# K and Q turned on VectorE instead of TensorE for the last pairs of a chunk-select attention followed by a hardswish MLP

## The chip, the cores and the metric

The kernel runs on one core of a Trainium2 chip. The metric is the device time of one execution in microseconds (us). A core has TensorE (PE; its weight loads are listed as PEld), VectorE (DVE), ScalarE (ACT), GpSimd (POOL) and SyncE (SP, which issues DMAs here). Each engine works through its own instructions in program order and waits for others by semaphores.

## The reference

Attention with selection of key chunks, over 4 batches of 8 heads with 768 positions and a head dimension of 64, and then an MLP with a hardswish gate over the 3072 tokens (512 to 2048 to 512). All arrays are float32.

```python
k_chunks = k.reshape(B, H, nc, chunk, D)                  # chunk = 32, nc = 24
k_min, k_max = np.min(k_chunks, axis=3), np.max(k_chunks, axis=3)
ub = np.sum(np.maximum(q[:, :, :, None, :] * k_min[:, :, None, :, :],
                       q[:, :, :, None, :] * k_max[:, :, None, :, :]), axis=-1)
ub = np.where(causal, ub, -1000000000.0)
top_chunks = np.argsort(ub, axis=-1)[..., -top_k:]        # top_k = 6
scores = scale * np.matmul(q, k.transpose(0, 1, 3, 2))
mask = sel & (pos[:, None] >= pos[None, :])               # sel: key's chunk is a top chunk
attn = softmax(np.where(mask, scores, -1000000000.0))
x = np.matmul(attn, v)                                    # heads side by side: [3072, 512]
h = x @ w_in
out = (h * np.clip(h + 3.0, 0.0, 6.0) / 6.0) @ w_out
```

The bound of a query and a chunk can be computed by two matrix products, since max(q kmin, q kmax) = relu(q) kmax - relu(-q) kmin.

## The kernel before

**Tiling.** Two heads of a batch form a pair, 16 pairs in all (i = 0 to 15, four per batch). The two heads (e = 0, 1) of 64 dimensions stand on the upper and lower 64 partitions. Queries below 192 (Q0) see at most six chunks and need no selection; the other 576 (NQ) are handled in two halves h of 288 (HQ). The MLP works on 8 groups g of 384 tokens, two per batch.

**Order.** The whole schedule is a list of tokens, ORDER, written out by hand; each token emits a few instructions, and every engine runs its share of the list in that order. The tokens, with the line under which the profile shows their instructions:

- lk, lq, lv: loads of K, Q, V of a pair, issued on SP (K and Q: L215, two DMAs each, rows of 256 bytes, 768 rows per DMA). K and Q each have a ring of three buffers (KSM, QS).
- K.i.c, Q.i.c: six TensorE transposes of 128x128 float32 blocks into a PSUM slot a, b or c (L298). kb, qb: casts to bf16 on ACT (L319, L329). mx, mn: maximum and minimum per chunk on DVE, into KM (L344). rp: relu(q) on ACT (L350). rn or ra: relu(-q), on DVE (L354) or ACT (L358).
- U, or ud for two pairs at once: the bounds by matmul (L367, L391); ub or us: add the causal bias on DVE, into UBM (L372, L396). ud.6, ud.8, ud.10, ud.12, ud.14 each serve two pairs.
- T: TensorE transposes of the bounds into PSUM slot x or y (L403, L408); t8: twelve DVE instructions, each finding the eight largest of 32 (L413); sel: compare with the sixth largest (L417); L: TensorE transposes back (L427); mt: copy the mask rows to MTM (L431, L436).
- Pairs 0 to 5 add the mask to the scores by matmul (L479, with EM holding E_VAL). Pairs 6 to 15 store it to DRAM (sm, L444, four DMAs) and load it spread over partitions (ml, L449, six DMAs), cut it causally on POOL (am, L456), and multiply the exponentials by it on DVE (mu, L463).
- S, ex: scores on TensorE (L471), exponential on ACT (L485). af: causal cut on POOL (L492).
- A, B: products with V into slot x or y (L508), na, nb: divide by the sum on DVE, into XB (L525, L528).
- xt: DMA transposes of XB to XT on SP (L534), three per group; groups 0 and 1 use TensorE (X, L541) and a DVE copy (xe, L545) instead.
- H.g.f.c: first MLP product into a slot a, b or c (L552), hu: relu(h + 3) on ACT (L560), gt: min with 6 and multiply by h on DVE (L563), which frees the PSUM slot. O.g.t.n: second product into slot x or y (L590), ot: copy out on ACT (L597), st: store on SP (L603).

PSUM has three slots of two banks (a, b, c: PBa, PBb, PBc in the profile) and two of one bank (x, y: PSx, PSy). A slot is written again only when its reader is through.

Of the kernel before, what the change touches and what calls it, by code (L numbers as in the profile page):

```python
# [15 lines left out]
P = 128  # L16
# [3 lines left out]
E_VAL = 8192.0  # L20
# [15 lines left out]
Q.1.b T.0.x mn.1 t8.0 sel.0 lq.2 Q.2.a lk.2 lv.0 lq.3 lk.3 lv.1 rp.1 qb.1 ra.1 U.1.c ub.1 lk.4 vc.0 lv.2 lq.4  # L36
rp.2 qb.2 ra.2 K.2.b kb.2 L.0.y mt.0 S.0.1.c ex.0.1 S.0.2.a T.1.x S.0.3.c ex.0.2 ex.0.3 S.0.5.a ex.0.5 mx.2 mn.2
S.0.0.b ex.0.0 t8.1 sel.1 U.2.c ub.2 S.0.4.a ex.0.4 L.1.y Q.3.b rp.3 mt.1 S.1.1.c ex.1.1 qb.3 T.2.x t8.2 rn.3
K.3.a kb.3 af.0.5 af.0.3 af.0.0 af.0.1 A.0.y S.1.0.c ex.1.0 mx.3 sel.2 mn.3 S.1.4.b ex.1.4 S.1.2.c ex.1.2 L.2.x
S.1.5.b ex.1.5 vc.2 af.0.2 S.1.3.a ex.1.3 U.3.c mt.2 S.2.2.b ex.2.2 S.2.0.a ex.2.0 af.1.0 na.0 af.1.1 ub.3 T.3.x  # L40
t8.3 af.1.3 sel.3 af.2.2 af.1.5 K.4.c lq.5 kb.4 mx.4 S.2.3.b Q.4.a ex.2.3 B.0.0.y L.3.x mt.3 rp.4 lk.5 wl.0 lv.4
lq.7 S.2.1.b ex.2.1 vc.1 wc.0 af.2.0 af.1.2 af.2.1 B.0.1.y qb.4 mn.4 A.1.x S.3.1.b ex.3.1 S.3.2.c ex.3.2 S.2.5.b
ex.2.5 rn.4 U.4.a nb.0 S.3.0.c ex.3.0 na.1 ub.4 S.2.4.b ex.2.4 T.4.y t8.4 sel.4 K.5.a kb.5 mx.5 S.3.5.c ex.3.5
Q.5.b B.1.0.x L.4.y rp.5 mt.4 qb.5 B.1.1.x mn.5 S.4.2.c af.3.0 ex.4.2 rn.5 A.2.y lv.3 S.3.3.a ex.3.3 af.2.5 lk.7
lk.6 lq.8 lq.6 vc.3 wl.2 S.4.1.b U.5.c na.2 nb.1 ub.5 ex.4.1 vc.4 af.3.2 af.2.3 S.4.3.a ex.4.3 af.4.3 af.3.5
af.3.3 bd af.3.1 S.4.4.b ex.4.4 wc.2 af.4.1 af.4.2 T.5.y S.4.0.c S.3.4.a B.2.0.x S.4.5.b ex.4.0 ex.4.5 af.4.0
af.4.5 t8.5 sel.5 ex.3.4 L.5.y mt.5 B.2.1.x nb.2 lv.5 S.5.1.c ex.5.1 S.5.2.b X.0.0.y A.3.x na.3 xe.0.0 K.6.a
wl.1 lk.8 af.5.1 wc.1 ex.5.2 lk.9 wl.4 kb.6 mx.6 S.5.3.c ex.5.3 Q.6.b mn.6 B.3.0.x X.0.1.y xe.0.1 rp.6 qb.6
B.3.1.x rn.6 S.5.5.c ex.5.5 nb.3 K.7.a kb.7 mx.7 S.6.1.b ex.6.1 mn.7 Q.7.c X.1.0.y rp.7 qb.7 rn.7 S.5.0.b
B.4.0.x B.4.1.x nb.4 ex.5.0 S.6.2.a ex.6.2 af.5.2 wl.3 S.7.0.c S.5.4.b A.4.x ex.5.4 ud.6.a S.6.0.b xe.1.0 na.4  # L50
ex.7.0 us.6 X.1.1.y S.7.1.c ex.6.0 xe.1.1 lq.9 T.7.x t8.7 S.6.4.a ex.7.1 ex.6.4 S.6.3.b ex.6.3 T.6.y sel.7 t8.6
sel.6 H.1.2.c hu.1.2 gt.1.2 af.5.0 af.5.3 af.5.5 af.7.0 S.6.5.a ex.6.5 af.7.1 vc.5 af.6.0 H.1.3.b L.6.x L.7.y
mt.6 mt.7 hu.1.3 gt.1.3 K.8.a wc.4 wl.6 kb.8 wc.3 wc.6 Q.8.c rp.8 qb.8 A.5.x B.5.0.y mx.8 mn.8 rn.8 H.1.0.b
hu.1.0 gt.1.0 K.9.a kb.9 mx.9 mn.9 H.0.1.c hu.0.1 gt.0.1 B.5.1.y H.1.4.b hu.1.4 H.1.1.a hu.1.1 sm.6 Q.9.c rp.9
gt.1.4 qb.9 gt.1.1 wl.5 rn.9 sm.7 ml.6.1 wc.5 af.6.1 ml.6.4 ml.6.3 lv.6 vc.6 am.6.4 H.0.6.b hu.0.6 gt.0.6 na.5
H.0.5.a hu.0.5 ud.8.c us.8 H.0.4.b gt.0.5 wl.7 T.8.x t8.8 ml.6.0 ml.6.5 am.6.3 wc.7 ml.6.2 lk.10 lk.11 hu.0.4
gt.0.4 nb.5 S.8.0.c ex.8.0 H.0.0.a ml.7.5 am.6.5 am.6.2 hu.0.0 gt.0.0 H.0.2.c hu.0.2 gt.0.2 H.0.3.b S.7.3.a
T.9.y hu.0.3 lq.10 ml.7.4 ml.7.2 ml.7.3 sel.8 gt.0.3 H.0.7.c ex.7.3 t8.9 hu.0.7 mu.6.5 gt.0.7 ml.7.1 lq.11
S.7.4.a ex.7.4 S.8.3.b ex.8.3 O.0.0.0.x O.0.0.1.x am.7.3 am.7.5 am.7.2 am.7.4 ml.7.0 S.7.2.a S.8.4.c S.8.5.b
# [36 lines left out]
H.5.2.b hu.5.2 O.3.0.0.y O.3.0.1.y ml.14.2 gt.5.1 B.12.0.x B.12.1.x gt.5.2 nb.12 S.15.2.c ex.15.2 S.15.0.a
S.15.1.b am.14.2 O.3.0.2.y ex.15.0 ex.15.1 B.13.0.x B.13.1.x ml.15.2 ml.15.5 ml.15.0 S.15.3.c ex.15.3 ml.14.5
# [17 lines left out]
def kernel(  # L115
# [536 lines left out]
```

## Time and profile before

| | us |
|---|---|
| Time, median of 2 runs (lowest, highest) | 282.94 (282.64, 283.25) |
| Span of the profiled execution | 282.4 |
| PE / DVE / ACT / POOL busy in it | 271.8 / 195.1 / 182.1 / 72.1 |
| Six K or Q transposes on PE, in the chain | 0.66 to 0.84 |
| 12 DVE maxima of 32 (mean of one, overlapped) | 1.27 (0.177) |
| DVE select, 96x384 | 0.55 |
| Landing of a K or Q load, median | 5.0 |

The granted TensorE clock is 1.00 throughout. Matmuls are pipelined, so a busy PE is not PE at its peak: the mean of one matmul contains time in which the one before it still runs. Engine idle time is listed with what ended it. The chain that ended last is followed back from the last instruction, at each step to what released it.

### The profile page before, as it was taken

The numbers are of one execution on the slowest core, as the hardware profiler recorded it, in microseconds if no ns is written. First come the engines' busy times: TensorE is split into PE (matmuls) and PEld (weight loads), VectorE is DVE, ScalarE is ACT, GpSimd is POOL, SyncE is SP. The second block draws the span as 40 slices with busy tenths as digits, with TensorE's granted clock in tenths as the row PEclk, the third lists the DMA queues.
The fourth block names the chain that finished last, engine by engine and source line by source line (L and its number), as shares of the span: only waits on it lengthen the run. The fifth ranks groups of instructions, "written<-read, shape, count | busy, mean of one in ns | idle before, by whom it ended". The sixth has DMA issues, their size and how long they took to land.

```text
span 282.4 us, 6943 instructions
## 1 busy us (share of the span) xinstructions
PE 271.8 (96%) x2706; PEld 164.7 (58%) x2706; DVE 195.1 (69%) x523; ACT 182.1 (64%) x242; POOL 72.1 (26%) x138
## 2 busy tenths in 40 slices
PE   8798999899999999998999999999999999999995
PEld 3566777757654666564556566645456646555544
DVE  4787786979898896568975798737935894532330
ACT  2699999988758988452888865753657433433331
POOL 6034294486254031005531120107004100000000
PEclk9999999999999999999999999999999999999999
DMA  8999999979979998599999789998789320111023
GB/s 167 218 201 214 269 218 245 281 230 311 272 227 284 245 195 195 150 273 264 251 278 207 146 183 206 257 294 164 206 255 267 97 40 37 39 56 62 15 75 111
DMA packets 107056, 54.39 MB, mean 193 GB/s; under 512 B 86928, under 2 KB 96144, under 8 KB 107024
## 3 DMA queue, kind: packets, MB, share of 16 engines
q1 hardware_dynamic: 105456, 53.56, 77.8%
q10 hardware_dynamic: 1568, 0.39, 0.7%
q8 instruction: 21, 0.34, 0.6%
q14 instruction: 11, 0.09, 0.1%
HBM read 42.34 MB, written 9.24 MB: 183 GB/s over the span
## 4 chain that ended last, share of the span: by engine, by line
PE 73%; DMA 8%; ACT 5%; SPq 5%; DVE 4%; issue 2%; POOL 1%; ACTq 0%
PE PSy L590 13%; PE PSx L590 11%; PE PBb L552 10%; PE PBa L552 8%; PE PBc L552 8%; ACT PT L485 4%; DMA WS<-in_moe_w_in_dram 3%; PE PSx L508 3%; DMA QS<-in_q_dram 3%; DMA KSM<-in_k_dram 3%; PE PSy L508 2%; PE PBa L298 2%; PE PBc L471 2%; SPq L449 2%; PE PBb L290 2%; PE PBa L471 2%
## 5 line engine op out<-in xcount | busy, mean ns | idle before, releaser
L552 PEld LDWEIGHTS <-WIN 128*128 128x128 bf16 x512 | 48.9, 98 | 32.8 <-issue 1.3
L590 PEld LDWEIGHTS <-GT 128*128 128x128 bf16 x368 | 34.4, 98 | 37.9 <-issue 2.5
L590 PE MATMUL PSy<-WOUT,GT 128*128 128x512 bf16 x208 | 50.5, 379 | 0.0
L590 PE MATMUL PSx<-WOUT,GT 128*128 128x512 bf16 x160 | 38.9, 379 | 0.0
L552 PE MATMUL PBb<-XT,WIN 128*128 128x384 bf16 x192 | 35.1, 326 | 0.0
L485 ACT ACTIVATE PT<-PBc 128x1024 bf16<-128x1024 f32 (+2 forms) x34 | 31.4, 924 | 3.9 <-PE PBc L471 3.2
L485 ACT ACTIVATE PT<-PBb 128x1024 bf16<-128x1024 f32 (+2 forms) x35 | 31.3, 895 | 3.8 <-PE PBb L471 2.0
L456 POOL TENSOR_SCALAR_AFFINE_SELECT WS<-WS 128x256 bf16<-128x256 bf16 x30 | 12.5, 427 | 71.6 <-DMA WS<-SCR 51.8
L560 ACT ACTIVATE U<-PBb 128x768 bf16<-128x768 f32 x24 | 19.5, 811 | 16.3 <-PE PBb L552 16.3
L552 PE MATMUL PBa<-XT,WIN 128*128 128x384 bf16 x160 | 29.3, 326 | 0.0
L563 DVE SCALAR_TENSOR_TENSOR GT<-U,PBb 128x768 bf16<-128x768 bf16 x24 | 22.8, 950 | 9.4 <-ACT U L560 9.1
L552 PE MATMUL PBc<-XT,WIN 128*128 128x384 bf16 x160 | 29.3, 326 | 0.0
L508 PEld LDWEIGHTS <-PT 128*128 128x128 bf16 x672 | 24.8, 98 | 6.1 <-POOL PT L492 1.7
L463 DVE TENSOR_TENSOR PT<-PT,WS 128x256 bf16<-128x256 bf16 (+2 forms) x70 | 27.4, 441 | 0.0
L485 ACT ACTIVATE PT<-PBa 128x1024 bf16<-128x1024 f32 (+2 forms) x27 | 25.8, 954 | 2.0 <-PE PBa L471 1.3
L563 DVE SCALAR_TENSOR_TENSOR GT<-U,PBa 128x768 bf16<-128x768 bf16 x20 | 19.0, 950 | 10.6 <-ACT U L560 10.5
L563 DVE SCALAR_TENSOR_TENSOR GT<-U,PBc 128x768 bf16<-128x768 bf16 x20 | 19.0, 950 | 10.4 <-ACT U L560 10.4
L492 POOL TENSOR_SCALAR_AFFINE_SELECT PT<-PT 128x256 bf16<-128x256 bf16 x56 | 22.2, 420 | 11.6 <-ACT PT L485 11.5
L560 ACT ACTIVATE U<-PBa 128x768 bf16<-128x768 f32 x20 | 16.3, 813 | 13.5 <-PE PBa L552 13.3
L293 POOL CAST VB<-VS 128x768 bf16<-128x768 f32 x16 | 13.5, 850 | 44.5 <-DMA VS<-in_v_dram 44.5
L471 PEld LDWEIGHTS <-KB 64*128 64x128 bf16 x320 | 14.4, 94 | 14.6 <-issue 10.3
L560 ACT ACTIVATE U<-PBc 128x768 bf16<-128x768 f32 x20 | 16.2, 812 | 9.9 <-PE PBc L552 9.6
(125 smaller groups left out, 396.3 us busy)
## 6 DMA issues: line engine op xcount, KB each, us to landing
VS<-in_v_dram SPq DMA_DIRECT2D x16, 384.0 KB, 5.0
KSM<-in_k_dram SPq DMA_DIRECT2D x31, 192.0 KB, 5.0
QS<-in_q_dram SPq DMA_DIRECT2D x31, 192.0 KB, 5.0
out_dram<-OT SPq DMA_DIRECT2D x23, 256.0 KB, 2.3
WS<-in_moe_w_in_dram SPq DMA_DIRECT2D x4, 1024.0 KB, 8.6
WS<-in_moe_w_out_dram SPq DMA_DIRECT2D x4, 1024.0 KB, 6.2
SCR<-MTM SPq DMA_DIRECT2D x40, 72.0 KB, 3.5
WS<-SCR SPq DMA_DIRECT2D x10, 288.0 KB, 5.5
```

The source lines that it names most:

```text
L290: nc.tensor.matmul(PSB[c][:, 0, :], lhsT=WARM[:, 0:P], rhs=WARM, start=True, stop=True)
L293: nc.gpsimd.tensor_copy(VB[i % 4][:, :, :, 0:D], VS[i % 2][:].rearrange("p e j d -> p j e d"))
L456: nc.gpsimd.affine_select(out=T, in_=T, pattern=[[0, 2], [1, P]], compare_op=A.is_ge, fill=0.0, base=0, channel_multiplier=-1)
L463: nc.vector.tensor_tensor(out=T, in0=T, in1=mask_view(i, j, lo, q0 + n), op=A.mult)
L471: nc.tensor.matmul(PSB[c][:, e, at:at + n], lhsT=K[rows, j * P:(j + 1) * P], rhs=Q[rows, q0:q0 + n], start=True, stop=q0 + n <= Q0 or i in ...
L485: nc.scalar.activation(PT[i % 3][u][:, :, 0:n], PSB[slot["S", i, u]][:, :, 0:n], ACT.Exp, scale=float(scale))
L492: nc.gpsimd.affine_select(out=T[:, :, lo:lo + P], in_=T[:, :, lo:lo + P], pattern=[[0, 2], [1, P]], compare_op=A.is_ge, fill=0.0, base=0, ...
L508: nc.tensor.matmul(O[:, e, t, :], lhsT=PT[i % 3][u][:, e, lo:lo + P], rhs=VB[i % 4][:, j, e, :], start=(j == 0), stop=(j == qb))
L552: nc.tensor.matmul(PSB[c][:, ff, 0:GRP], lhsT=WIN[:, kt, (2 * f + ff) * P:(2 * f + ff + 1) * P], rhs=XT[g % 3][:, kt, :], start=(kt == 0), ...
L560: nc.scalar.activation(slot["R", g, f][:], PSB[slot["H", g, f]][:, :, 0:GRP], ACT.Relu, bias=3.0)
L563: nc.vector.scalar_tensor_tensor(out=GT[g % 2][:, 2 * f:2 * f + 2, :], in0=slot["R", g, f][:], scalar=6.0, in1=PSB[slot["H", g, f]][:, :, ...
L590: nc.tensor.matmul(PSS[c][:], lhsT=GT[g % 2][:, f, t * P:(t + 1) * P], rhs=WOUT[:, f, :], start=(f == 0), stop=(f == FT - 1))
```

## The change

K and Q of pairs 10 to 15 (tokens kd, qd in place of K, Q) are loaded by load_turned: four DMAs per tensor, each to 32 partitions, in rows of 32 float32 (128 bytes), so that a DVE transpose of 32x32 blocks, in place in SBUF, gives the layout that TensorE gave before. The casts and reductions then read SBUF instead of PSUM. For these pairs the second part of the bound is q times the minimum (negation dropped), and the first is relu(q) times the maximum less the minimum, for which kx subtracts the two on DVE; relu(-q) is no longer made. The K casts of pairs 11, 13 and 15 go from ACT to POOL (kp).

For pairs 6 to 15 the selection of two pairs at once stays on DVE: tr (block transpose of the bounds, 128x576), tm (18 maxima instead of 24), se (one compare), tb (block transpose of the mask). The tokens T, t8, sel, L and mt of these pairs go. tr, tm, se and tb stand directly behind us of their pair of pairs. Everything else in ORDER keeps its place; kd and qd stand where K and Q stood.

For pairs 0 to 5, E_VAL and the compare change sign, so that mt is a plain copy.

```diff
-E_VAL = 8192.0
+E_VAL = -8192.0
...
-ex.7.0 us.6 X.1.1.y S.7.1.c ex.6.0 xe.1.1 lq.9 T.7.x t8.7 S.6.4.a ex.7.1 ex.6.4 S.6.3.b ex.6.3 T.6.y sel.7 t8.6
-sel.6 H.1.2.c hu.1.2 gt.1.2 af.5.0 af.5.3 af.5.5 af.7.0 S.6.5.a ex.6.5 af.7.1 vc.5 af.6.0 H.1.3.b L.6.x L.7.y
-mt.6 mt.7 hu.1.3 gt.1.3 K.8.a wc.4 wl.6 kb.8 wc.3 wc.6 Q.8.c rp.8 qb.8 A.5.x B.5.0.y mx.8 mn.8 rn.8 H.1.0.b
...
+S.7.0.c S.5.4.b A.4.x ex.5.4 ud.6.a S.6.0.b xe.1.0 na.4 ex.7.0 us.6 tr.6 tm.6.0 tm.6.1 se.6 tb.6 X.1.1.y S.7.1.c
+ex.6.0 xe.1.1 lq.9 S.6.4.a ex.7.1 ex.6.4 S.6.3.b ex.6.3 H.1.2.c hu.1.2 gt.1.2 af.5.0 af.5.3 af.5.5 af.7.0 S.6.5.a
+ex.6.5 af.7.1 vc.5 af.6.0 H.1.3.b hu.1.3 gt.1.3 K.8.a wc.4 wl.6 kb.8 wc.3 wc.6 Q.8.c rp.8 qb.8 A.5.x B.5.0.y mx.8
...
+sm.6 Q.9.c rp.9 gt.1.4 qb.9 gt.1.1 wl.5 rn.9 sm.7 ml.6.1 wc.5 af.6.1 ml.6.4 ml.6.3 lv.6 vc.6 am.6.4 H.0.6.b hu.0.6
+gt.0.6 na.5 H.0.5.a hu.0.5 ud.8.c us.8 tr.8 tm.8.0 tm.8.1 se.8 tb.8 H.0.4.b gt.0.5 wl.7 ml.6.0 ml.6.5 am.6.3 wc.7
+ml.6.2 lk.10 lk.11 hu.0.4 gt.0.4 nb.5 S.8.0.c ex.8.0 H.0.0.a ml.7.5 am.6.5 am.6.2 hu.0.0 gt.0.0 H.0.2.c hu.0.2
...
+ex.8.2 mu.6.4 O.0.1.0.y H.1.7.b hu.1.7 A.6.x na.6 kd.10 kd.11 gt.1.7 kb.10 kp.11 mx.10 mx.11 mn.10 kx.10 mn.11 kx.11
+B.6.0.x O.0.1.1.y qd.10 O.0.1.2.y O.0.1.3.y B.6.1.x rp.10 qb.10 ot.0.1 st.0.1 sm.8 st.0.0 lk.12 nb.6 S.9.3.a S.9.5.c
+S.9.2.b ex.9.3 mu.7.4 mu.7.3 mu.7.1 mu.7.0 ex.9.5 ex.9.2 O.0.2.0.y O.0.2.1.y qd.11 O.0.2.2.y rp.11 qb.11 O.0.2.3.y
+S.9.4.c ex.9.4 ot.0.2 ud.10.b S.9.0.a S.9.1.c lv.8 ex.9.1 mu.7.2 mu.7.5 ex.9.0 sm.9 A.7.x B.7.0.y us.10 tr.10
+tm.10.0 tm.10.1 se.10 tb.10 na.7 xt.2 B.7.1.y st.0.2 nb.7 S.10.1.c ex.10.1 S.10.4.b S.10.0.a ml.9.2 ml.8.3 ml.8.1
...
+    def load_turned(dst, x, i):
+        b, hp = divmod(i, NPAIR)
+        for e in range(2):
+            for d in range(2):
+                g = D * e + CH * d
+                nc.sync.dma_start(dst[g:g + CH].rearrange("p (n d) -> p n d", d=CH),
+                                  x[b, 2 * hp + e].rearrange("(n t) d -> t n d", t=CH)[:, :, CH * d:CH * (d + 1)])
...
+    def turn_k(i):
+        nc.vector.transpose(out=KF[i % 3], in_=KF[i % 3])
...
+    def k_span(i):
+        T = KM[i % 3][:, :, 0:NCH]
+        nc.vector.tensor_tensor(out=T[:, 0], in0=T[:, 0], in1=T[:, 1], op=A.subtract)
...
+    def turn_double(i):
+        nc.vector.transpose(out=UBT[:], in_=UBD.rearrange("p e n -> p (e n)"))
+
+    def top8_double(i, e):
+        view = UBT[:].rearrange("p (s c) -> p s c", c=CH)
+        for s in range(9 * e, 9 * e + 9):
+            nc.vector.max(out=T8D[:, s, :], in_=view[:, s, :])
+
+    def select_double(i):
+        nc.vector.tensor_tensor(out=SELD[:], in0=UBT[:].rearrange("p (s c) -> p s c", c=CH),
+                                in1=T8D[:, :, TOPK - 1:TOPK].to_broadcast([P, 2 * HQ // CH, CH]),
+                                op=A.is_ge if i in PRODUCT else A.is_lt)
+
+    def turn_back(i):
+        nc.vector.transpose(out=MTD[(i // 2) % 2].rearrange("p e n -> p (e n)"), in_=SELD[:].rearrange("p s c -> p (s c)"))
```

## The prediction

> **What bounds the kernel now.** I read the page first: engine totals and slices.
>
> ```profile
> PE 271.8 (96%) x2706; PEld 164.7 (58%) x2706; DVE 195.1 (69%) x523; ACT 182.1 (64%) x242; POOL 72.1 (26%) x138
> ...
> PE   8798999899999999998999999999999999999995
> ...
> DVE  4787786979898896568975798737935894532330
> ...
> DMA  8999999979979998599999789998789320111023
> ```
>
> PE is occupied everywhere, DMA until slice 31 (about 220 us). The chain that ended last agrees (73% PE), but it leaves PE in two places that the change touches, waiting for the loads of Q 12 and K 13:
>
> ```profile
> 123.20 0.54 SPq L215
> 123.80 7.47 DMA QS<-in_q_dram
> 131.41 0.84 PE PBb L298 x6
> ...
> 144.78 7.13 DMA KSM<-in_k_dram
> 152.04 0.84 PE PBa L298 x6
> ```
>
> PE stood still only 0.80 and 0.15 us there, so PE's work and the loads arrive nearly together: taking PE work away gains little unless the load comes earlier too. Then the timeline around the four places where the change puts selection work on DVE in one piece. Columns: start, length, engine, line, operation.
>
> ```profile
> 60.91 0.76 DVE L396 TENSOR_TENSOR UBM<-PBa,BIASM 128x576 f32<-128x576 f32 x1 [0.57 <-PE PBa L391]
> ...
> 61.58 0.55 DVE L545 COPY XT<-PSy 128x768 bf16<-128x768 bf16 x1
> ...
> 63.09 1.46 PE L552 MATMUL PBc<-XT,WIN 128*128 128x384 bf16 x8
> ...
> 79.80 0.76 DVE L396 TENSOR_TENSOR UBM<-PBc,BIASM 128x576 f32<-128x576 f32 x1
> ...
> 80.47 0.94 DVE L563 SCALAR_TENSOR_TENSOR GT<-U,PBa 128x768 bf16<-128x768 bf16 x1
> ...
> 81.68 1.47 PE L552 MATMUL PBa<-XT,WIN 128*128 128x384 bf16 x8
> ```
>
> Each time the bias add (us) is followed on DVE at once by something PE needs within two microseconds: the last copy into XT before H.1.2, and the gate that frees PBa for H.0.0. At 108.38 (us.10) the two normalisations follow, the second at 110.36; PSy is written again at 113.60 (O.1.2.0).
>
> **What goes.** On PE, 12 groups of six K or Q transposes at 0.66 us (their pieces in the chain), 10 groups T at 0.35 (starts 159.77, 160.14, 160.47) and 10 groups L at 0.13 (165.67, 165.80, 165.92): 7.9 + 3.5 + 1.3 = 12.7 us. On ACT, five negative parts (0.67) and three K casts (0.80): 5.8 us; the casts go to POOL, 0.85 each by its row for VB. On DVE, 10 x (12 maxima 1.27 + select 0.55 + mask 0.30) = 21.2 us and one negative part, 0.76.
>
> **What comes on DVE.** No row shows a block transpose. Of 128x768 f32 I bound it by the 128x768 bf16 copy, 0.55 us, and by twice the 128x768 f32 reduction, 1.9; I take the reduction's own 0.95, the same shape passed once. Selection of a double pair: transpose of 128x576 f32 0.76 (the row of us; bounds 0.42 to 1.5), 18 maxima at 0.105 (12 took 1.27) 1.9, select 0.76, bf16 transpose 0.45 (between copies of 288, 0.30, and of 768, 0.55): 3.9 us in one unbroken block. Five blocks, 19.5, replace the 21.2; twelve turns add 11.4 and six subtractions of 24 columns 0.6. DVE's total rises by about 10 us; that is not the point. The point is where each piece stands in DVE's order.
>
> Costed at nothing: the casts on POOL for pairs 11 and 15 (POOL is 26% busy; the scores of these pairs come several us later; without that cover 0.85 each), the source of casts and reductions (SBUF for PSUM: the PSUM rows stand, 0.80 and 0.95; a gain is possible, of a tenth or so by their pace), and the sign in pairs 0 to 5 (mask row 0.30 as copy, 0.305 with the subtraction). ACT's 5.8 us are a gain only where ACT is waited for; at pair 10 it is, and the wait for DVE there is longer.
>
> [...]
>
> **What comes on the queues.** Each of 12 loads is four DMA issues instead of two. An issue of 768 packets takes about 0.55 us on SP (1.12 for two at 123.20): +1.1 us of SP per tensor. Packets double to 3,072 and halve to 128 bytes. From 5 to 10 us only 256-byte packets run:
>
> ```profile
> DMA packets 4338, 1.09 MB, mean 218 GB/s; under 512 B 4338, under 2 KB 4338, under 8 KB 4338
> ```
>
> That is 5 us x 16 / 4338 = 18.4 ns of an engine per packet. Rows of 2 KB reach some 430 GB/s near 53 us, 76 ns per packet. A line through both gives 14.3 ns for 128 bytes: 2.75 us per tensor against 1.77. The bounds are 1.77 (cost by bytes) and 3.53 (cost by packets). I take the middle between 1.77 and the line, about +0.5 us, for the sum and the rest for the range.
>
> [...]
>
> **The sum, against the profiled span of 282.4** (the runs' median, 282.94, is 0.5 above it). I follow the order through and say by how much PE is late (+).
>
> Pair 6/7: us.6 ends 61.67, block to 65.6, xe.1.1 to 66.1; H.1.2 starts there instead of 63.09: +3.0; L.6, L.7 gone: +2.7. Until then PE has only two groups of scores, under 1 us.
>
> Pair 8/9: us.8 ends 83.3, block to 87.2, gt.0.5 to 88.1; H.0.0 needs PBa: 88.1 instead of 81.68, +6.4. T.9, L.8, L.9 gone: +5.8 at A.6.
>
> Turns of 10 and 11: na.6 ends at 103.0 (97.22 before). Then in order on DVE kd.10, kd.11 (1.9), gt.1.7 (0.95), four reductions (3.6), two subtractions (0.2), qd.10 (0.95): 110.6. ACT waits in order at rp.10 for that, then qb.10, then ot.0.1, which frees PSy: 112.7; O.0.2.0 starts there instead of 102.46. PE's saved 2.0 us (K.10, K.11, Q.10) is lost in the wait. ud.10 needs qd.11 and rp.11: 116.3 instead of 107.0, +9.3. The loads are covered: lk.10 and lk.11 are issued from 83.58 on and need some 3 us longer than before, kd.10 comes at 103. Were that cover gone, each late microsecond would add one.
>
> Pair 10/11: us.10 ends 118.4, block to 122.3, na.7 and nb.7 to 123.8; O.1.2.0 at 123.8 instead of 113.60, +10.2. xt.2 waits for na.7, so H.2.7 is equally late.
>
> Q 12: SP goes on from xt.2 (issue ends 127.0) through one store and nine mask loads (6.6 us as before) and four issues (2.2) to 135.8; the load lands 7.5 us later, 143.3; qd.12 ends 144.3. PE no longer waits for it, but na.8 and gt.2.5 queue behind it on DVE, and B.8 and S.11.5 behind those: +9.
>
> K 13: lq.13 costs SP 1.1 more; lk.13 is issued with +10 and +1.1 more, lands at about 164 (152.0 before); kd.13, then kp.13 on POOL, 165.8; S.13.0 was at 153.96: +11.8. ud.12 some +11.5.
>
> Pair 12/13: us.12 ends 170.2, block to 174.1, na.11 to 174.9; xt.4 must wait for na.11, 3.8 of issue, 2.5 to land: 181.2. H.4.0 was at 167.22: +14.
>
> Pairs 14, 15: SP issues 17 DMAs in place of 9 (8.3 us before), kd.15 waits for the last; gt.4.4 and O.4.2.2 queue behind kd.15, two reductions, qd.15, kd.14. 2.65 us of PE is saved, and about as much lost in these waits. T and L of these pairs (0.96) go, and block 14 is covered by O.4.1, H.3.7, H.3.4 and O.4.0 (some 8 us of PE): +13. From 215 us on nothing changes and PE is full, so the delay reaches the end: 282.9 + 13 = about 296.
>
> Of the 13, the four blocks give 3.0, 3.7, 1 and 2.5 (10), the turns of 10/11 3.5, the later loads about 3.5; 4 come back as saved PE work. With turns at 0.55 us, blocks at 3.1 and packets at no more than their bytes, the same walk gives +7, 290; with turns and blocks' transposes doubled and packets at full price, +24, 307.
>
> **Rivals.** *PE is relieved (faster).* The end is set by PE in 73% of the chain; 12.7 us of its work goes, to 270. It needs DVE's blocks to be hidden: DVE is 31% idle, but at 61, 80 and 109 us the follower is wanted within 2 us. It decides if a block takes under 2 us. *Paid back (no change).* The waits of about 13 use up the 12.7 once: 283; for it speaks that PSUM banks a to c come free earlier and PE finds work at the blocks; against, that PE's order is fixed. *128-byte packets set it (slower still).* At 3.53 us per tensor or more and DMA full from 120 to 155, the late loads of 12, 13, 14 and 15 add 6 to 8: 303. *It doesn't do what it says:* a 4-byte turn takes two passes, 1.9 us; DVE then holds ud.10, Q 12, K 13 and 15 some 9 us longer: 305. This one is in the upper range.
>
> **The numbers.** My walk 0.60, packets or two-pass turns 0.16, paid back 0.15, relieved 0.09. The likeliest gives 296. The range 284 to 308 takes in the bounds of the unknown costs and the upper part of "paid back". About 2% is what a measurement here can tell from no change: slower 0.77 (nearly all of the first two), same 0.14, faster 0.09.
>
> **What would show it.** H.1.2 starting 3 us after the last maximum of pair 6, H.0.0 right behind a gate that follows tb.8; PE idle of several microseconds near 63, 84, 105, 118 and 178; ACT waiting for DVE at rp.10; DVE waiting for a load at qd.12, kd.13, kd.15; turns in rows of 0.95 us; loads of K and Q with over 5 us to land. I'm wrong if PE goes on without gaps at 62 to 66, or if the turns cost less than half.

## The result and the profile after

The changed kernel takes 310.03 us (median of 309.46 and 310.60) against 282.94: a ratio of 1.0978, 95% interval 1.0877 to 1.1079. The direction was forecast, the size was not: +27 us came where +13 was expected, 2 us above the upper end of the range. The profiled execution has a span of 307.7 us (before 282.4) and a mean granted clock of TensorE of 0.967 (before 1.000). The kernels below are compared with up to 17 runs of the kernel before, median 282.5. Executions of one kernel mostly spread by 1 to 5 us, so differences of one microsecond between times are not read.

From the page of the changed kernel, engine totals and slices (each 7.7 us):

```profile
PE 269.2 (87%) x2554; PEld 155.3 (50%) x2574; DVE 207.4 (67%) x505; ACT 177.2 (58%) x234; POOL 75.6 (25%) x141
...
PE   8798999939949956989879897949999999999995
...
DVE  3777887866895497684986887894785496342430
...
PEclk9999999978997995999999999997999999999999
DMA  9999999989989703749899956979978840030112
```

PE has four holes (slices 9, 12, 15 and 27, counted from 1), and the row PEclk, which was all nines before, drops in or right after each of them. The busy time of PE fell by only 2.6 us, though 12.7 us of its work was taken out. Most of the rest went into slower matmuls: the granted clock is at half for 20.5 us in all (65.3 to 72.1, 92.6 to 96.0, 116.5 to 123.3 and 208.7 to 212.1), and PE works in 17.1 of them, which loses 8.5. After slice 28 PE is full, as before.

The four holes in the timeline of PE (start, length, operation, in brackets the idle time before it and its releaser):

```profile
67.06 2.08 PE L556 MATMUL PBc<-XT,WIN 128*128 128x384 bf16 x6 [4.82 <-DVE XT L549]
...
91.63 1.79 PE L556 MATMUL PBa<-XT,WIN 128*128 128x384 bf16 x8 [4.25 <-DVE GT L567]
93.22 2.77 PE L556 MATMUL PBc<-XT,WIN 128*128 128x384 bf16 x8
...
118.17 4.42 PE L594 MATMUL PSy<-WOUT,GT 128*128 128x512 bf16 x10 [5.00 <-ACT OT L601]
...
207.82 2.81 PE L594 MATMUL PSy<-WOUT,GT 128*128 128x512 bf16 x8 [4.16 <-DVE GT L567]
```

The releasers are those of the prediction: the copy into XT behind block 6, the gate behind block 8, ot.0.1 behind the turn of Q 10, gt.4.4 behind the turns of pairs 14 and 15. For the last two, the rows of ScalarE and VectorE show the turns ahead of them (rp.10 waits for the turn, ot.0.1 follows at 117.53; a turn, then gt.4.4):

```profile
116.22 0.68 ACT L337 ACTIVATE RP<-QS 128x576 f32<-128x576 f32 x1 [5.72 <-DVE QS L239]
...
205.99 0.93 DVE L236 STREAM_TRANSPOSE KSM<-KSM 128x768 f32<-128x768 f32 x1
206.85 0.91 DVE L567 SCALAR_TENSOR_TENSOR GT<-U,PBb 128x768 bf16<-128x768 bf16 x1
```

The lengths of the matmuls are not as predicted: eight of an H group took 1.46 to 1.47 us before and take 2.77 at 93.22. The windows of 5 us show it as the granted clock (the column with no count, 0.53 and so on, after the busy times of PE, PEld, DVE, ACT and POOL):

```profile
65.00:70.00 5.00, 2.94 (x10) 1.10 (x10) 1.97 (x3) 0.83 (x2) 2.50 (x2) 0.53 0.70 253
70.00:75.00 5.00, 5.00 (x52) 3.65 (x50) 2.83 (x4) 3.40 (x5) 1.89 (x1) 0.79 0.79 245
...
115.00:120.00 5.00, 1.83 (x5) 0.69 (x5) 4.93 (x13) 3.78 (x6) 0.00 (x0) 0.65 0.16 57
120.00:125.00 5.00, 4.95 (x32) 1.82 (x35) 0.94 (x3) 2.25 (x4) 0.00 (x0) 0.67 0.61 142
```

And the first hole from the side of VectorE, with GpSimd's row that lies beside it. The block is 60.82 to 66.56, 5.74 us where 3.9 was costed:

```profile
60.82 0.78 DVE L395 STREAM_TRANSPOSE UBT<-UBM 128x576 f32<-128x576 f32 x1
61.63 1.77 DVE L400 MAX8 T8D<-UBT 128x8 f32<-128x32 f32 x18
63.44 2.31 DVE L403 TENSOR_TENSOR SELD<-UBT,T8D 128x576 bf16<-128x576 f32 x1
65.78 0.78 DVE L408 STREAM_TRANSPOSE MTM<-SELD 128x576 bf16<-128x576 bf16 x1
66.48 0.52 DVE L549 COPY XT<-PSy 128x768 bf16<-128x768 bf16 x1
...
63.25 1.89 POOL L252 CAST WOUT<-WS 128x2048 bf16<-128x2048 f32 x1
```

How late PE is against the profile before, read from the first weight load of matmul groups that both kernels have (us):

| place | predicted | after |
|---|---|---|
| H.1.3 and H.1.1, behind block 6 | +3.0 | +4.7, +5.9 |
| O.0.0.0, behind block 8 | +6.4 | +11.5 |
| O.0.2.3, behind the turns of 10 and 11 | +10.2 | +17.3 |
| O.1.2.0, behind block 10 | +10.2 | +17.5 |
| O.2.2.0, behind Q 12 | +9 | +20.1 |
| O.2.1.1, behind K 13 | +11.8 | +20.4 |
| H.4.5, behind block 12 | +14 | +22.0 |
| O.3.1 and all that follows | +13 | +25.0 |

Two things lie under all such figures. Within the first 10 us, where the kernels are the same, the profiles already differ by up to 1.3 us (against the profile before: changed kernel +0.3, filled stalls −0.5, one stall +0.1, one stall filled −1.0). And the profile before waits 1.3 us for GpSimd at 57 us, which most others don't, so that they seem some 1.1 us less late than they are. Growth from row to row is free of both; where two runs are compared below, the difference of their starts is named.

The theory to be tested after this: the stalls are the predicted ones, but each long one is paid twice, once as waiting and once in the half-rate matmuls after it. The rivals: the 128-byte loads, or VectorE too full as such.

### The profile page after: what moved, and what is told of

It reads as the page before. It is cut to its first block, busy times and chain, and to the rows that moved or that the text cites. A ratio compares the mean times of both kernels' runs of the same rounds, so it can differ in the third digit from the quotient of the medians.

```text
span 307.7 us, 6684 instructions
## 1 busy us (share of the span) xinstructions
PE 269.2 (87%) x2554; PEld 155.3 (50%) x2574; DVE 207.4 (67%) x505; ACT 177.2 (58%) x234; POOL 75.6 (25%) x141
## 4 chain that ended last, share of the span: by engine, by line
PE 51%; DVE 16%; issue 9%; ACT 8%; DMA 8%; SPq 5%; POOL 2%; DVEq 0%; ACTq 0%; POOLq 0%
PE PSx L594 8%; PE PSy L594 7%; PE PBa L556 7%; PE PBb L556 7%; PE PBc L556 6%; ACT PT L489 5%; DVE KM L329 4%; DMA VS<-in_v_dram 3%; SPq L220 3%; DVE GT L567 3%; PE PSx L512 2%; DMA out_dram<-OT 2%; PE PBb L286 2%; PE PSy L512 2%; DMA KSM<-in_k_dram 2%
## 5 line engine op out<-in xcount | busy, mean ns | idle before, releaser
L556 PEld LDWEIGHTS <-WIN 128*128 128x128 bf16 x512 | 50.1, 100 | 50.4 <-issue 19.2
L594 PEld LDWEIGHTS <-GT 128*128 128x128 bf16 x368 | 35.5, 100 | 54.3 <-issue 14.8
L594 PE MATMUL PSy<-WOUT,GT 128*128 128x512 bf16 x198 | 52.1, 400 | 11.0 <-ACT OT L601 5.0
L594 PE MATMUL PSx<-WOUT,GT 128*128 128x512 bf16 x150 | 37.9, 386 | 0.6 <-issue 0.2
L556 PE MATMUL PBb<-XT,WIN 128*128 128x384 bf16 x192 | 36.5, 335 | 0.6 <-ACT PT L489 0.5
L556 PE MATMUL PBc<-XT,WIN 128*128 128x384 bf16 x160 | 31.7, 343 | 5.5 <-DVE XT L549 4.8
L567 DVE SCALAR_TENSOR_TENSOR GT<-U,PBb 128x768 bf16<-128x768 bf16 x24 | 22.8, 948 | 12.5 <-ACT U L564 12.2
L460 POOL TENSOR_SCALAR_AFFINE_SELECT WS<-WS 128x256 bf16<-128x256 bf16 x30 | 12.9, 439 | 66.9 <-DMA WS<-SCR 66.8
```

The costliest lines, as they stand in the source:

```text
L460: nc.gpsimd.affine_select(out=T, in_=T, pattern=[[0, 2], [1, P]], compare_op=A.is_ge, fill=0.0, base=0, channel_multiplier=-1)
L556: nc.tensor.matmul(PSB[c][:, ff, 0:GRP], lhsT=WIN[:, kt, (2 * f + ff) * P:(2 * f + ff + 1) * P], rhs=XT[g % 3][:, kt, :], start=(kt == 0), ...
L567: nc.vector.scalar_tensor_tensor(out=GT[g % 2][:, 2 * f:2 * f + 2, :], in0=slot["R", g, f][:], scalar=6.0, in1=PSB[slot["H", g, f]][:, :, ...
L594: nc.tensor.matmul(PSS[c][:], lhsT=GT[g % 2][:, f, t * P:(t + 1) * P], rhs=WOUT[:, f, :], start=(f == 0), stop=(f == FT - 1))
```

## The experiments

**The change in two halves.** One run has only the selection's part, the other only the turned K and Q.

```diff
 # selection only: K, Q, their loads, casts and parts as before
-ud.6.a ... us.6 ... T.7.x t8.7 ... T.6.y sel.7 t8.6 sel.6
+ud.6.a ... us.6 tr.6 tm.6.0 tm.6.1 se.6 tb.6 ...
 # turning only: T, t8, sel, L, mt as before
-K.10.a K.11.c gt.1.7 kb.10 kb.11 mx.10 mx.11 mn.10 mn.11
+kd.10 kd.11 gt.1.7 kb.10 kp.11 mx.10 mx.11 mn.10 kx.10 mn.11 kx.11
```

> The kernel before with only the selection of pairs 6 to 15 moved to VectorE, in one block behind each bias add as in the change; K and Q of pairs 10 to 15 stay on TensorE. Theory (the blocks hold up what TensorE waits for, and each stall of over 4 us is followed by some 5 us at half the matmul rate): the two stalls before H.1.2 and H.0.0 come back with the slow matmuls behind them, 294 to 298 us. Rival (the 128-byte loads set the loss): no loss here, 278 to 284 us.

> The kernel before with only K and Q of pairs 10 to 15 turned on VectorE (128-byte loads, kd, qd, kx, casts on GpSimd); the selection stays on TensorE. Theory: the stalls before O.0.2.0 (pairs 10/11) and O.4.2.2 (pairs 14/15) remain, 290 to 297 us, and the two losses add up to the whole (27 us). Rival (each part alone finds slack and only both together lose): under 287 us.

Selection only: 298.4 us, ratio 1.061 (1.0543 to 1.0678), +16; the two stalls come back, 3.17 us before H.1.2 and 5.61 before H.0.0. Turning only: 294.9, ratio 1.0432 (1.0387 to 1.0476), +12.4, with stalls of 4.99 us before O.0.2.0 and 4.17 before O.4.2.2. Together they make 28.3, against 27 for the whole change: the halves add up, and the larger one is the selection, of which the prediction had said 10 less the work that PE is spared. Where each half is late: selection only is +3.2 at H.1.1, +9.8 at O.0.0.0, +11.2 at O.1.2.1 and +12.9 at H.4.5; turning only (its profile is of the longest of its four executions, 298.3 us) is ahead by about 2 until O.0.2.0, which is the difference of the starts and of the wait at 57 us alone, then +3 at O.0.2.1, +4.7 at O.2.2.0, +8.9 at O.2.1.3 and +13 from O.3.1 on.

**The same blocks, put later.** The whole change, with each block cut in pieces that stand behind the copy or gate that PE waits for.

```diff
-us.6 tr.6 tm.6.0 tm.6.1 se.6 tb.6 ... xe.1.1 ... gt.1.2
+us.6 ... xe.1.1 tr.6 tm.6.0 tm.6.1 ... gt.1.2 se.6 tb.6
-us.8 tr.8 tm.8.0 tm.8.1 se.8 tb.8 ... gt.0.5 ... gt.0.4 ... gt.0.0 ... gt.0.2 ... gt.0.3
+us.8 ... gt.0.5 tr.8 ... gt.0.4 tm.8.0 ... gt.0.0 tm.8.1 ... gt.0.2 se.8 ... gt.0.3 tb.8
```

Blocks 10 and 12 likewise, behind nb.7, gt.1.6 and gt.2.7, and behind na.11, gt.3.6 and gt.3.5; block 14 stayed.

> The changed kernel with the same instructions, the four blocks tr, tm, se, tb of pairs 6, 8, 10 and 12 cut into two to five pieces and moved behind the copy, gates and normalisations that TensorE waits for. Theory: the stalls before H.1.2 and H.0.0 and their slow matmuls go, 295 to 299 us. Rival (VectorE is simply too full, so the work costs the same wherever it stands): 306 us or more.

297.4 us, ratio 1.0499 (1.0437 to 1.0562): the place alone is worth some 12.5 us, since the instructions are the same. For the selection this speaks against the rival that VectorE is too full as such. The first two holes are gone, the other two stand:

```profile
108.10 2.26 PE L593 MATMUL PSy<-WOUT,GT 128*128 128x512 bf16 x5 [4.99 <-ACT OT L600]
...
195.18 3.60 PE L593 MATMUL PSy<-WOUT,GT 128*128 128x512 bf16 x8 [4.16 <-DVE GT L566]
```

**The clock: the holes filled.** Two runs put matmuls of constants into the holes, so that PE waits as long but is not idle.

```diff
+    def busy(c, n):
+        flat = EM[:].rearrange("p j h x -> p (j h x)")
+        for _ in range(n):
+            nc.tensor.matmul(PSS[c][:] if c in "xy" else PSB[c][:, 0, :], lhsT=IDENTB[:], rhs=flat[:, 0:512],
+                             start=True, stop=True)
...
-H.1.2.c ... H.0.0.a ... S.9.3.a S.9.5.c S.9.2.b ... O.0.2.0.y ... O.4.2.2.y
+ZX.x.22 H.1.2.c ... ZX.x.18 H.0.0.a ... ZX.c.22 S.9.3.a S.9.5.c S.9.2.b ... O.0.2.0.y ... ZX.a.18 O.4.2.2.y
```

That is the second of the two; in the first, the third set was 80 matmuls of 128 columns into slot c, directly ahead of O.0.2.0.

> The changed kernel with idle matmuls (identity by a constant, into columns of PSUM that nobody reads) put into the four long TensorE stalls, before H.1.2, H.0.0, O.0.2.0 and O.4.2.2. Theory (after 4 us of an idle TensorE its granted clock is halved for about 5 us): the stalls keep their length, the matmuls behind them run at full rate, 299 to 303 us. Rival (the slow matmuls come from what runs beside them, memory traffic or VectorE): they stay slow, 309 to 312 us.

It missed: 311.7 us, ratio 1.1042 (1.1009 to 1.1075), in the range of its rival, though the matmuls behind the first two holes ran at a clock of 1.00. At O.0.0.0 PE was only +6.15 late instead of +11.5 (1.0 of the difference is in the starts), but the third set had to wait 6.82 us for an exp that still read slot c, started at 114.60 and ran into the time when O.0.2.0 was free to go; +18.1 followed. The fill had become a delay of its own, so it was made again with that set ahead of S.9.3, where slot c is empty.

> The changed kernel with matmuls of constants (512 columns each, results never read) put into its four long stalls; unlike in the first try, the third set goes ahead of S.9.3 into slot c, which nothing is waiting to read there. Nothing of the reference is left out. Theory (a stall of PE of over 4 us makes the matmuls after it run at half rate, and this is 8 to 10 us of the 27): granted clock 1.00 throughout, 300 to 303 us, O.0.2.0 no later than +11 instead of +16. Rival (the slow matmuls do not lie on the path, since the waits behind them are for DVE, ACT and loads): 307 to 310 us, as the changed kernel.

Its four executions took 303.64 and 304.0 us at a granted clock of 1.00 and 0.994, and 310.99 and 312.7 at 0.983 and 0.978, so no ratio can be given: the fill kept the clock up in two of them, and why not in the other two is open. In the profiled one (303.64, span 301.9) the groups behind the first two holes run at full pace:

```profile
66.25 1.14 PE L562 MATMUL PBc<-XT,WIN 128*128 128x384 bf16 x6 [0.22 <-DVE XT L555]
...
88.44 1.46 PE L562 MATMUL PBa<-XT,WIN 128*128 128x384 bf16 x8 [0.26 <-DVE GT L573]
89.74 1.46 PE L562 MATMUL PBc<-XT,WIN 128*128 128x384 bf16 x8
```

1.14 us for six instead of 2.08, though the block ahead of them is as long as in the changed kernel (its select takes 2.32). PE is +6.75 at O.0.0.0 (after: +11.5), +10.25 at O.0.2.3 (+17.3), +19.1 at the end (+25.0). Of each difference 0.8 us is there before the first hole. The fourth fill gained nothing; a stall of 1.25 us for gt.4.4 stayed. So some 5 us of the 25 went with the clock in this execution. Because the executions differ, the same question was put to the kernel before, with one hole and nothing else.

```diff
+    def hold(n):
+        for _ in range(n):
+            nc.vector.tensor_reduce(out=IDLE[:], in_=BIASM[:].rearrange("p (c w) -> p c w", w=CH),
+                                    axis=AX.X, op=A.max)
...
-us.6 X.1.1.y S.7.1.c ex.6.0 xe.1.1
+us.6 X.1.1.y S.7.1.c ex.6.0 ZD.16 xe.1.1
 # in the twin also
-T.6.y ... H.1.2.c
+ZX.c.22 T.6.y ... H.1.2.c
```

> The kernel before with 16 reductions of a constant on VectorE (about 0.37 us each, their results never read) ahead of xe.1.1: one stall of TensorE of some 5 us at 62.7 us and nothing else; everything is computed. Theory (a stall of this length is followed by matmuls at half rate): the 8 matmuls of H.1.2 behind it take over 2.4 us instead of 1.46, TensorE is later by the stall and about 2 us more, 289 to 291 us. Rival (the stall alone counts): H.1.2 in 1.46 us, 287 to 288 us.

> As the run with one stall, with 22 matmuls of constants into slot c (4.8 us, results never read) where TensorE would stand still. Theory: H.1.2 in 1.46 us, granted clock 1.00 in the stretch, about 2 us less than its twin. Rival (the clock has no part in it): the same time as its twin.

The reductions took 7.78 us, 0.49 each instead of the expected 0.37, so the hole is longer than meant, 7.1 us. The stall alone and its window:

```profile
68.78 0.88 PE L407 MATMUL PSy<-IDENT,UBM 128*96 128x128 f32 x3 [7.08 <-DVE XT L549]
69.44 2.58 PE L556 MATMUL PBc<-XT,WIN 128*128 128x384 bf16 x8
...
65.00:70.00 5.00, 1.23 (x5) 0.90 (x6) 4.76 (x21) 0.00 (x0) 1.89 (x1) 0.50 0.66 223
```

And filled:

```profile
67.68 0.53 PE L412 MATMUL PSy<-IDENT,UBM 128*96 128x128 f32 x3 [2.23 <-DVE XT L554]
68.05 1.46 PE L561 MATMUL PBc<-XT,WIN 128*128 128x384 bf16 x8
...
65.00:70.00 5.00, 2.77 (x18) 1.35 (x16) 4.83 (x26) 0.45 (x1) 1.99 (x2) 1.00 0.72 229
```

The same eight matmuls take 2.58 and 1.46 us, the clock is 0.50 and 1.00. In these two profiles PE is +7.5 and +5.2 late at O.0.0, 2.3 us apart, but 1.1 us of that is there from the first 10 us on, so the clock costs 1.2. The times differ by as little: 291.3 us (290.96 to 291.42) against 290.3 (289.08 to 291.16), which by itself decides nothing. That one long hole halves the rate of the next matmuls is shown by the rows; the price is small and has a plain reading. The clock is at half from 64.9 to 71.7 us, and PE works only in the last 2.9 us of that, which loses 1.5. Behind the first hole of the changed kernel it works 5.1 us at half rate, which loses 2.5, and there the filled run gains 2.4 (at H.1.1 +5.9 against +2.8, less 0.8 of the starts). So a hole costs, beside its own length, about half of the time that PE works at half rate after it: worked out from the stretches above, 1.5 to 2.6 us for each hole here.

**The loads.** First the kernel before with 128-byte loads and nothing turned, then with as many issues but the old packets.

```diff
-            load(KS[i % 3], k, i)
+            (load_turned if i >= 10 else load)(KS[i % 3], k, i)
 # four issues:
+    def load_four(dst, x, i):
+        b, hp = divmod(i, NPAIR)
+        for e in range(2):
+            for h in range(2):
+                nc.sync.dma_start(dst[:, 3 * h:3 * h + 3, e, :],
+                                  x[b, 2 * hp + e, 384 * h:384 * h + 384].rearrange("(j p) d -> p j d", p=P))
```

> The kernel before, with K and Q of pairs 10 to 15 loaded by four DMAs each in rows of 128 bytes; TensorE turns them as before, so these pairs' K and Q are permuted and the values differ from the reference, while the work is the same in kind and number. Theory (rows of 128 bytes cost about half a microsecond per tensor and SP's issues one, which shows only at the waits for Q 12 and K 13): 284 to 288 us. Rival (the packets set the loss of the turned loads): 292 us or more, most of what the turning alone costs (294.9).

> The kernel before, with K and Q of pairs 10 to 15 loaded by four DMAs each (one per head and half of the rows) in rows of 256 bytes, as many packets as before; everything is computed. It tells apart what the loads in 128-byte rows alone cost, 292.1 us. If the number of SP's issues does it: 289 to 293 us. If the packets' number and size do it: 282 to 285 us, and the waits for Q 11, K 13 and K 15 that came with the 128-byte rows stay under half a microsecond.

128-byte loads alone: 292.1 us, ratio 1.0309 (1.0233 to 1.0384). Four issues alone: 287.0, ratio 1.0139 (1.0093 to 1.0184), and 285.3 in the one of its four executions whose clock stayed at 1.00. The first is nearer to its rival; the second lies between its two cases. So the loads cost some 9.6 us with nothing else changed, about 4.5 of it with the mere number of issues. PE's stalls in the run with 128-byte loads, whose profile is of the longest of its four executions (295.5 us):

```profile
105.28 0.85 PE L304 MATMUL PBa<-IDENT,QS 128*128 128x128 f32 x6 [1.84 <-DMA QS<-in_q_dram]
...
121.83 1.46 PE L558 MATMUL PBc<-XT,WIN 128*128 128x384 bf16 x8 [1.51 <-DMA XT<-XB]
...
156.88 0.85 PE L304 MATMUL PBa<-IDENT,KSM 128*128 128x128 f32 x6 [1.82 <-DMA KSM<-in_k_dram]
...
185.36 0.84 PE L304 MATMUL PBc<-IDENT,KSM 128*128 128x128 f32 x6 [1.86 <-DMA KSM<-in_k_dram]
```

These are Q 11, the first XT piece of group 2, K 13 and K 15; with four issues of 256-byte rows none of them is there. What stays with four issues is a wait that no one had listed: SP needs 11.2 us from the first issue of lk.14 to the last of lk.15 (before 8.3, with 128-byte rows 12.7; lv.13 among them), the store st.2.0 behind them goes out later, and ScalarE waits for that store's buffer before ot.4.1, in order ahead of three hu. In the run with four issues:

```profile
194.07 0.60 ACT L601 ACTIVATE OT<-PSx 128x512 f32<-128x512 f32 x1 [7.38 <-DMA out_dram<-OT]
...
194.72 0.29 PE L431 MATMUL PSx<-IDENTB,SEL 96*128 96x96 bf16 x3 [2.71 <-ACT OT L601]
```

The same row of the kernel before starts at 192.55 after 3.74 us of waiting. PE goes from −2.1 us at O.4.1.3 to +2.5 at O.4.0.3: 2.7 us are the stall, and most of the rest is a stretch of half clock behind it, from 196.1 to 199.5 us.

**The order around the turns.** Starting from the run with later blocks; first ot.0.1 and gt.4.4 are put ahead of the turns that held them, then the two waits that took their place are treated the same way.

```diff
 # first
-gt.1.7 kb.10 kp.11 mx.10 mx.11 mn.10 kx.10 mn.11 kx.11 B.6.0.x O.0.1.1.y qd.10 ... rp.10 qb.10 ot.0.1 ... nb.6
+gt.1.7 qd.10 mx.10 mn.10 kx.10 kb.10 kp.11 B.6.0.x O.0.1.1.y ... ot.0.1 nb.6 mx.11 mn.11 kx.11 rp.10 qb.10
-gt.4.3 qd.14 kd.15 O.4.1.0.x O.4.2.0.y H.4.4.b ... rp.14 qb.14 hu.4.4 ... kd.14 kb.14 gt.4.4
+gt.4.3 O.4.1.0.x O.4.2.0.y H.4.4.b hu.4.4 gt.4.4 qd.14 kd.15 ... rp.14 qb.14 ... kd.14 kb.14
 # then also
-kx.11 ... mu.7.4 mu.7.3 mu.7.1 mu.7.0 ... qd.11 ... rp.11 qb.11
+kx.11 qd.11 ... ex.9.2 rp.11 qb.11 ...
-qd.14 kd.15 ... rp.14 qb.14 mx.15 ... kd.14 kb.14
+qd.14 kd.14 kd.15 ... rp.14 qb.14 kb.14 mx.15 ...
```

> The changed kernel with the blocks moved behind what TensorE waits for (as in the run with later blocks, 297.4) and DVE's and ACT's order round the turns mended: qd.10 straight behind gt.1.7 and ot.0.1 ahead of rp.10, the reductions of pair 11 behind nb.6, hu.4.4 and gt.4.4 directly behind H.4.4, qd.14 and kd.15 behind gt.4.4. Theory (what is left of the loss there is the wait for ot.0.1 at O.0.2.0, some 5 us, and the wait for gt.4.4 at O.4.2.2, some 4): 286 to 291 us, no stall of over 3 us at those two places. Rival (DVE is too full by the turns themselves, and each move only shifts the wait to na, nb and gt): 295 us or more.

> The run with the order mended (294.9 us) with qd.11, rp.11 and qb.11 moved ahead of the mask products of pair 7, and kd.14 and kb.14 ahead of the reductions of pair 15. Theory (its two last stalls, 4.1 us for rp.11 at the bounds of pair 10 and 4.2 us for kb.14 at S.14.1, are of order alone): 287 to 290 us; what stays are the loads, about 5. Rival (the waits move on to the next in line): 293 us or more.

First 294.9 us, ratio 1.0407 (1.033 to 1.0485), then 293.6, ratio 1.0397 (1.0346 to 1.0449). Both miss; the second lies in the range of its rival, the first just under it. The two stalls that the first was made for are gone, and it has two others, of 4 us:

```profile
109.78 0.70 PE L378 MATMUL PBb<-RP,KM 64*32 64x288 f32 x4 [4.10 <-ACT RP L336]
...
194.35 0.39 PE L474 MATMUL PBb<-QB,KB 64*128 64x256 bf16 x2 [4.19 <-ACT KB L315]
```

In the second the first of these is 0.83 us, but at the other place the wait moved from kb.14 to kx.14, which now came last on VectorE:

```profile
193.95 1.22 PE L378 MATMUL PBa<-RP,KM 64*32 64x288 f32 x16 [4.00 <-DVE KM L333]
```

There the rival is right: a gate, four turns and two pairs of reductions stand in one queue from 185 to 194 us, and PE needs something from each end of it.

**Is there a kernel faster than both?** Selection only, with the blocks as in the run with later blocks, but block 8's select behind gt.0.7 and block 10 spread over gt.1.5, gt.1.6 and mn.12; then with Q 12, Q 13 and K 13 loaded earlier and tm.8.1 behind gt.0.7.

```diff
 # first, against selection only in the old places
-us.8 tr.8 tm.8.0 tm.8.1 se.8 tb.8 ... gt.0.5 ... gt.0.4 ... gt.0.0 ... gt.0.7
+us.8 ... gt.0.5 tr.8 ... gt.0.4 tm.8.0 ... gt.0.0 tm.8.1 ... gt.0.7 se.8 tb.8
-us.10 tr.10 tm.10.0 tm.10.1 se.10 tb.10 ... nb.7 ... gt.1.5 ... gt.1.6 ... mn.12 ... gt.2.7
+us.10 ... nb.7 tr.10 ... gt.1.5 tm.10.0 ... gt.1.6 tm.10.1 ... mn.12 se.10 ... gt.2.7 tb.10
 # then also
-xt.2 ... st.0.2 ... ml.9.2 ml.8.3 ml.8.1 ml.9.5 ml.8.0 ml.8.5 ml.8.4 ml.8.2 ml.9.4 lq.12
+xt.2 ... st.0.2 lq.12 ... ml.9.2 ml.8.3 ml.8.1 ml.9.5 ml.8.0 ml.8.5 ml.8.4 ml.8.2 ml.9.4
-sm.11 ... lq.13 ... st.1.1 lk.13
+lq.13 lk.13 sm.11 ... st.1.1
```

> The kernel before with the selection of pairs 6 to 15 turned by VectorE, no turned K or Q and the loads as before, and the blocks in pieces behind what TensorE waits for. Theory (the blocks cost 16 us by their place alone, and what they take off TensorE, 4.8 us, is then a gain): 279 to 284 us, no stall of over 2 us, granted clock 1.00. Rival (VectorE's selection in itself is too slow for the masks' way through DRAM): 287 us or more, with the loss at S.7, S.9 or S.11.

> The run with the selection later (283.6 us) with tm.8.1 behind gt.0.7, the load of Q 12 ahead of the mask loads of pairs 8 and 9 and those of Q 13 and K 13 ahead of the mask stores of pair 11. Theory (what TensorE was spared, 5.2 us by the page, is lost in the waits for Q 12, 0.9 us, and K 13, 0.7, for gt.0.2, 1.1, and in small ones): 280 to 282 us, under the kernel before. Rival (the masks that the loads are put ahead of, or the XT transposes, come late instead): 283 us or more.

Selection only, later: 283.6 us, ratio 1.0037 (1.0004 to 1.0069), as fast as before within what can be told, with 15 us less than the same instructions in the old places. PE has 5.2 us less to do and ends no sooner:

```profile
PE 266.6 (94%) x2626; PEld 159.9 (57%) x2646; DVE 195.2 (69%) x488; ACT 182.2 (64%) x242; POOL 72.3 (26%) x138
...
131.28 0.84 PE L294 MATMUL PBb<-IDENT,QS 128*128 128x128 f32 x6 [0.88 <-DMA QS<-in_q_dram]
...
152.76 0.84 PE L294 MATMUL PBa<-IDENT,KSM 128*128 128x128 f32 x6 [0.73 <-DMA KSM<-in_k_dram]
```

With the loads earlier: 286.7, ratio 1.0099 (1.0053 to 1.0145), a miss. In the profiled execution (287.55 us) Q 12 and K 13 are no longer waited for, but masks are, of those that the loads were put ahead of; VectorE waits for one, and PE for VectorE's product:

```profile
151.47 0.36 DVE L467 TENSOR_TENSOR PT<-PT,WS 128x384 bf16<-128x384 bf16 x1 [4.49 <-DMA WS<-SCR]
...
151.89 0.48 PE L512 MATMUL PSy<-VB,PT 128*128 128x65 bf16 x10 [3.46 <-DVE PT L467]
```

Of its twelve executions four took 283.4 to 283.8 at a clock of 1.00 and the others 286 to 288 at 0.992 to 0.998; where the longer ones lose it beyond the one stretch of half clock in the profile is open. No version tried is faster than the kernel before.

## Why the prediction was right in direction and wrong in size

*Right.* The places: block 6 before xe.1.1, block 8 before gt.0.5, ot.0.1 behind rp.10, gt.4.4 behind the turns of 14 and 15 are the four holes. The last was named, but priced at no net loss (+14 to +13), and took +22 to +25. The rows that no trace had shown (groups: line, operation, count, then busy time and mean in ns):

```profile
L239 DVE STREAM_TRANSPOSE QS<-QS 128x768 f32<-128x768 f32 x6 | 5.8, 972 | 0.0
L236 DVE STREAM_TRANSPOSE KSM<-KSM 128x768 f32<-128x768 f32 x6 | 5.6, 952 | 0.0
...
L395 DVE STREAM_TRANSPOSE UBT<-UBM 128x576 f32<-128x576 f32 x5 | 3.9, 779 | 0.2
L408 DVE STREAM_TRANSPOSE MTM<-SELD 128x576 bf16<-128x576 bf16 x5 | 3.9, 778 | 0.2
```

0.95 was costed for the turn, 0.76 for the f32 transpose; the bf16 one was costed at 0.45 and takes as long as the f32 one. A block that nothing disturbs is 0.78 + 1.77 + 0.76 + 0.78 = 4.1 us, against 3.9. The rows of 0.95 rule out the two-pass turn, and with it one of the ways to 305. The packets' own time is right too: the main queue's share of 16 engines times the span is 219.7 us before and 225.9 after, 6.2 us over 12 tensors or 0.52 each, against "+0.5 us". The run with 128-byte loads alone gives 226.1 and the one with four issues of the old rows 217.1, so 0.52 is good to some 0.2.

*The step that failed* is the sum: "Of the 13, the four blocks give 3.0, 3.7, 1 and 2.5 (10), the turns of 10/11 3.5, the later loads about 3.5; 4 come back as saved PE work." Terms were missing in it or mis-sized. The points below overlap and are not shares that add up to the missing 12 us.

1. *The halved clock after a long stall* has no term at all. The walk moved every group by the wait ahead of it and kept its length. The filled run is 7.1 us less late than the changed kernel at O.0.2.3 and 5.8 at the end, each with 0.8 of the starts in it: some 5 of the missing 12 (25.0 against 13), of the 8.5 that PE loses at half clock. In the changed kernel the stalls of 4.16 us and more were followed by half-rate matmuls; those of 1.26 to 1.64 us were not. Over all the traces, every stall of 3.17 us and more was; of those between 1.8 and 2.8 us some were (1.81 with turning only, 2.15 with 128-byte loads, 2.31 in the first filled run, 2.71 with four issues) and some not (1.84, 2.23, 2.67). In the changed kernel's profile the four stretches of half clock last 6.83, 3.41, 6.83 and 3.41 us; by the windows of the first filled run and of the one with one stall they last 6.8 and 3.4, and 6.8. Between 1.81 and 2.71 us the length of the stall did not decide it; behind the one of 3.17 us in the selection-only run six matmuls took 1.61 us instead of 1.14.

2. *Block 6 was longer than a block.* Its select took 2.31 us instead of 0.76: 1.55 us. This is seen in the traces, and was not varied in a run of its own. In all six places of the traces where the select starts during a weight cast of GpSimd (here at 63.44, cast 63.25 to 65.14; with later blocks at 64.50, cast 63.18 to 65.07, and at 86.17, cast 86.05 to 87.94; one each in three other runs), it ends 0.6 us after the cast does, and so takes 0.89 to 2.39 us. The same 0.6 us behind the end stand where it starts during a cast of V (two places) or a causal cut (three; in a fourth, behind the cut that followed at once). Beside no such work it takes 0.75 to 0.76, and where it came first, at 62.40 in the first run with filled stalls, the cast took 2.31 us instead of 1.89. Before, the select read PSUM, and 0.55 us was all it took beside the same cast:

```profile
65.36 0.55 DVE L417 TENSOR_TENSOR SEL<-PSy,T 96x384 bf16<-96x384 f32 x1
...
64.23 1.89 POOL L256 CAST WOUT<-WS 128x2048 bf16<-128x2048 f32 x1
```

The change moved the select from one PSUM and one SBUF input to two in SBUF, and the prediction costed it by an add from PSUM. That the second SBUF input is what makes it wait is not shown: its shape changed too, from 96x384 to 128x576.

3. *Saved work does not come back.* The prediction let 4 us return. In the run with selection only, later, no stall is over 1.3 us, PE has 5.2 us less to do and ends at the same time; it waits instead for Q 12, K 13 and gates, and when these loads came earlier, for masks. For the whole change no run shows this by itself. It is the rival "paid back", right for its half of the change and with the blocks put elsewhere.

4. The *loads* were sized right as transfers and wrong as waits. By themselves they cost 9.6 us, where the sum had 3.5, through Q 11, XT, K 13, K 15 and the store ahead of ot.4.1. "The loads are covered" held for lk.10 and lk.11; lq.11 was not looked at. In the changed kernel part of this hides behind the larger stalls: its lateness from O.1.2.0 on grows by 7.5 us (17.5 to 25.0) where 2.8 was predicted. How much of those 4.7 us is loads and how much is VectorE's queue at pairs 12 to 15 is not settled; the runs with the order changed show that both are there.

The rival "128-byte packets set it" was right about the loads' weight and only half right about the packets: nearly half of it comes with issues alone. "PE is relieved" fell at the first hole.

## What to carry to other kernels

Where PE sets the end, price a wait by its length and, if it is long, add what the next matmuls may lose at half rate: here every stall of 3.17 us and more was followed by it, and some of 1.81 to 2.71 us, at up to 2.6 us for each hole. Blocks of 4 us on another engine were cheap in pieces of 1 to 2 us and dear in one (297.4 against 310.0 us). Moving 5.2 us of work from PE to VectorE gained nothing here (283.6 us against 282.5) where the transfers and gates that arrive just in time came no earlier, so look at the waits of under a microsecond first: they become the bound. The added DMA issues were paid by what stood behind them on the queue, a store and the engine waiting for its buffer included (ScalarE's wait for it 7.38 us instead of 3.74, the time 287.0 instead of 282.5). And before lateness is compared between two profiles, look how far apart they are where the kernels are still the same: here that was 1.1 of the 2.3 us between the two kernels with one hole.

## What the runs showed of the hardware

- VectorE's 32 x 32 block transpose takes 0.78 us for 576 columns and 0.95 to 0.97 for 768 in f32, 0.9 to 1.0 ns for each further column; for 576 columns of bf16 it takes 0.78 too.
- A select with both operands in SBUF that started during a GpSimd weight cast ended 0.6 us after the cast and so took 0.89 to 2.39 us instead of 0.76; the select before, with one operand in PSUM, took 0.55 us beside such a cast, as elsewhere.
- Halving the rows of the loads to 128 bytes cost 0.52 us of DMA time per 384 KB tensor at the same total of bytes, less than the waits that the 128-byte loads, with their four issues, caused: 9.6 us in the time for 12 tensors.
- The granted clock of TensorE went to half in stretches of 3.41 or 6.83 us (the four of the changed kernel): with every stall of 3.17 us and more, with some of 1.81 to 2.71 and with none below. A stretch began anywhere from 3.9 us before the end of its stall (the one of 7.08 us) to 1.4 us behind it (2.71 us).
